# Earlier token sums for the second group and a rebuilt lead-in in a fused attention and two-MoE kernel

## The chip, the cores and the metric

One core of a Trainium2 chip. The metric is the device time of one execution in microseconds (us); lower is better. TensorE is PE in the profile (PEld is its weight load), VectorE is DVE, ScalarE is ACT, GpSimd is POOL, and SP is the engine that here only issues DMAs.

## What is computed

Attention over 2 batches and 8 heads (576 positions, 64 values per head), mixed with the answer of a compressive memory, then two feed-forward layers. All of it is fp32.

```python
# q, k, v: 2 x 8 x 576 x 64, causal
local = softmax(q @ k.T / 8, causal) @ v
mem = (phi(q) @ M_prev) / (phi(q) @ z_prev + 1e-6)     # phi(x) = elu(x) + 1
x = g * mem + (1 - g) * local                          # g = sigmoid(beta), per head
x = x.reshape(1152, 512)                               # tokens x model
x = elu(x @ w_in) @ w_out                              # 512 -> 2048 -> 512
p = probs / (probs.sum(-1) + 1e-9)                     # 1152 x 4
out = sum(p[:, e] * (relu(x @ w1[e]) @ w2[e]) for e in range(4))   # 512 -> 1024 -> 512
```

## The kernel before

**Numbers.** Every fp32 factor of a product is held as a high and a low part (fp32r), and a product is three matmuls, high times high, low times high and high times low (`mm3`, L273 to L276). Making the parts is work for the other engines: ACT copies the high part and POOL (for weights and many activations) or DVE subtracts it from the value.

**Two groups of tokens.** Group 0 has 384 tokens (the first 192 positions of both batches), group 1 has 768. The attention of group 0 is four units F0 to F3, one for each pair of heads; that of group 1 is eight units R00 to R31, one for each pair of heads and batch. Group 0 goes through both feed-forward layers with plain products: `Moe1` (tiles `ua`, `ha`, `da`) and `Moe2` (`ub`, `hb`, `db`). Group 1 goes through them as `Wide1` and `Wide2`, which save products in the first halves by working with sums of token quarters and of weight quarters. The token sums T1 to T4 of the first layer come from class `Halves`: eight DVE subtractions (L713), eight high parts on ACT (L697) and eight low parts on POOL (L700). Products with them go to PSUM banks named `pa10A`, `pa10S` and so on.

**Order in time.** The lead-in holds F0 to F3. Then group 0's `Moe1` runs on PE, with the R units interleaved, then group 0's `Moe2` and the remaining R units, then group 1.

**Weights.** Group 0's `Moe1` takes blocks 0 to 15 from a 64-bit format that is converted on the chip (`plan_weights`, L188). Each block has two halves of 512 columns. SP loads a half into a raw buffer (tags `w64_0` and `w64_1`, two buffers each), ACT works on it (`upper`, L221) and writes a PSUM bank `cv`, DVE shifts there (`shift`, L227) and combines the raw half with the bank into the fp32 tile `wr` (`lower`, L231). ACT then makes `wh` (L241), POOL makes `wl` (L245), and SP stores `wr` in DRAM for later (`keep`, L237). Block 0 (`W_EARLY = 1`) uses a bank of pool `m` and may start at once; later ones use the score banks `s0` and `s1` and wait until the last scores of F3 are issued (`GATE`).

**What sets the order.** Class `Plan` (L1033) takes every step with an engine, an estimated cost, a rank, the steps it follows and the buffers it takes and gives; `order()` sorts each engine's instructions by that. `STARTS2` sets the ranks of the R units. Where the plan expects PE to wait, `keep_busy` (L307) puts matmuls with zeros in front of a step (L300), which write a bank that the step overwrites; `FEWEST` sets a least number for the F units.

**Buffers.** Pool `ap` holds the attention's SBUF tiles, `hp0` the `h`, `ev` and `acc` tiles of group 0, `hp1` those of group 1 and the T sums with their parts. `hp1` is opened after the block that holds all of group 0, in the memory of the pools closed there.

**Small things.** `gates` (DVE, after a DMA and ACT's `gate_e`) makes g; `probs` (DVE, L137 to L140) makes p. In a unit, the local sums' quotient (L1210, L1424, L1216), the addition `both` (L1402), the transposes `turn` (L1408) and the split of the result into `xh` (L1418) and `xl` (L1416) follow one another; with F3's, the first `ua` product can start.

## Time and profile before

| what | us |
|---|---|
| median of 3 runs (734.55 to 735.07) | 734.72 |
| the profiled execution | 736.48 |
| its span in the trace | 734.70 |
| outside the span | 1.78 |
| PE busy in the span | 722.6 (98%) |
| PE idle in the span | 12.1 |

The mean granted clock of PE is 0.991 of full speed. The profiled execution was 1.76 us above the median. A stage can be read by a window: busy time of each engine in it, the granted clock and the share of time that the DMA engines worked. The stages here are the lead-in (0 to 43.6), group 0's `Moe1` (43.6 to 143.4), the rest of group 0 (to 352.15) and group 1 (to the end).

### The profile page before, as it was taken

What the parts mean: (1) busy time and instruction counts of PE and PEld (TensorE: products, weight loads), DVE (VectorE), ACT (ScalarE), POOL (GpSimd) and SP (SyncE); (2) the same over time, 40 slices, a digit from 0 to 9 for tenths busy, and PEclk for the clock granted to TensorE, in tenths of its full rate; (3) what the DMA queues carried; (4) which work ended last, traced back from release to release, by engine and by line L of the source; (5) the groups of instructions that cost most, each with busy time, mean ns of one, the idle gap of its engine ahead of it and who ended that gap; (6) DMA issues with size and microseconds to landing.
All of it is one profiled execution on the core that took longest, in us unless ns stands there. A gap on an engine that the chain in (4) does not pass through costs nothing.

```text
span 734.7 us, 11055 instructions
## 1 busy us (share of the span) xinstructions
PE 722.6 (98%) x4263; PEld 647.8 (88%) x4263; DVE 391.9 (53%) x845; ACT 352.9 (48%) x609; POOL 425.8 (58%) x256
## 2 busy tenths in 40 slices
PE   9998999999999999999899999999999999999997
PEld 5788988989788788898799999998989989899896
DVE  4675976443542443532755584864636446364562
ACT  7667877553443542443577473753424324242230
POOL 5457668756446452356998665397666456664210
PEclk9899999999999999999899999999999999999999
DMA  8378897433141230322233121212312213021002
GB/s 259 109 245 320 307 323 248 156 114 126 40 162 63 75 124 17 112 87 70 93 115 107 54 95 49 67 30 87 115 29 87 78 37 115 28 89 57 1 1 86
DMA packets 23540, 80.36 MB, mean 109 GB/s; under 512 B 2880, under 2 KB 2880, under 8 KB 23488
## 3 DMA queue, kind: packets, MB, share of 16 engines
q1 hardware_dynamic: 23488, 79.66, 32.6%
q8 instruction: 33, 0.54, 0.3%
q14 instruction: 19, 0.16, 0.1%
HBM read 68.90 MB, written 10.75 MB: 108 GB/s over the span
## 4 chain that ended last, share of the span: by engine, by line
PE 88%; DMA 4%; ACT 3%; DVE 2%; POOL 1%; issue 1%; SPq 0%; DVEq 0%; ACTq 0%
PE db L274 9%; PE db L276 9%; PE db L275 9%; PE sums L1361 5%; PE da L274 4%; PE da L276 4%; PE da L275 4%; PE ub L274 4%; DMA w<-in_w 3%; PE ub L276 3%; PE ub L275 3%; PE sR L1283 2%; PE tR L1345 2%; PE sums L1370 2%; PE sums L1231 1%; DMA wmem<-in_beta 1%
## 5 line engine op out<-in xcount | busy, mean ns | idle before, releaser
L245 POOL TENSOR_TENSOR wl<-wr,wh 128x1024 fp32r<-128x1024 f32 x72 | 171.8, 2391 | 171.5 <-ACT wh L241 124.2
L241 ACT ACTIVATE wh<-wr 128x1024 fp32r<-128x1024 f32 x72 | 75.7, 1055 | 94.2 <-PE db L275 60.8
L274 PE MATMUL db<-wh,hb 128*128 128x512 f32 x288 | 115.0, 399 | 0.0
L276 PE MATMUL db<-wl,hb 128*128 128x512 f32 x288 | 112.8, 392 | 0.0
L275 PE MATMUL db<-wh,hb 128*128 128x512 f32 x288 | 112.6, 391 | 0.0
L990 DVE SCALAR_TENSOR_TENSOR acc<-db,pr,acc 128x512 f32<-128x512 f32 x42 | 31.5, 751 | 70.0 <-PE db L276 69.2
L274 PE MATMUL da<-ha,wh 128*128 128x384 f32 x192 | 65.7, 342 | 0.0
L276 PE MATMUL da<-ha,wh 128*128 128x384 f32 x192 | 64.6, 336 | 0.8 <-POOL ha L405 0.8
L276 PEld LDWEIGHTS db<-wl,hb 128*128 128x128 f32 x288 | 54.1, 188 | 11.7
L275 PE MATMUL da<-ha,wl 128*128 128x384 f32 x192 | 64.4, 335 | 0.0
L274 PEld LDWEIGHTS db<-wh,hb 128*128 128x128 f32 x288 | 54.2, 188 | 11.0 <-issue 0.3
L275 PEld LDWEIGHTS db<-wh,hb 128*128 128x128 f32 x288 | 54.2, 188 | 10.3
L274 PE MATMUL ub<-yh,wh 128*128 128x384 f32 x128 | 45.9, 358 | 0.0
L276 PE MATMUL ub<-yl,wh 128*128 128x384 f32 x128 | 43.0, 336 | 0.0
L275 PE MATMUL ub<-yh,wl 128*128 128x384 f32 x128 | 43.0, 336 | 0.0
L1352 ACT ACTIVATE pfR<-tR 128x512 f32<-128x512 f32 x24 | 14.3, 594 | 49.3 <-PE tR L1345 49.3
L1361 PE MATMUL sums<-rvR,pfR 128*128 128x65 f32 x288 | 37.5, 271 | 0.0
L533 DVE SCALAR_TENSOR_TENSOR acc<-db,pr,acc 128x512 f32<-128x512 f32 x21 | 15.8, 751 | 40.4 <-PE db L276 40.1
L276 PEld LDWEIGHTS da<-ha,wh 128*128 128x128 f32 x192 | 36.0, 188 | 1.5 <-POOL ha L405 1.4
L502 ACT ACTIVATE hb<-ub 128x384 fp32r<-128x384 f32 x32 | 15.7, 491 | 43.7 <-PE ub L276 43.7
L274 PEld LDWEIGHTS da<-ha,wh 128*128 128x128 f32 x192 | 36.1, 188 | 0.6 <-issue 0.2
L1361 PEld LDWEIGHTS sums<-rvR,pfR 128*128 128x128 f32 x288 | 35.3, 191 | 1.2 <-DVE tmR L1216 0.2
(881 smaller groups left out, 1880.0 us busy)
## 6 DMA issues: line engine op xcount, KB each, us to landing
wr<-in_w SPq DMA_DIRECT2D x64, 512.0 KB, 3.5
w<-in_w SPq DMA_DIRECT2D x32, 512.0 KB, 5.8
wscr<-wr SPq DMA_DIRECT2D x16, 512.0 KB, 7.0
wr<-wscr SPq DMA_DIRECT2D x16, 512.0 KB, 3.4
qkR<-in_qk_r SPq DMA_DIRECT2D x8, 480.0 KB, 5.2
rvR<-in_vm_r SPq DMA_DIRECT2D x8, 390.0 KB, 3.1
out<-acc SPq DMA_DIRECT2D x8, 256.0 KB, 2.0
qkF<-in_qk_f SPq DMA_DIRECT2D x4, 416.0 KB, 3.6
```

The lines of the kernel that those rows point to most:

```text
L241: nc.scalar.activation(out=t["wh"], in_=t["wr"], func=AF.Copy)
L245: nc.gpsimd.tensor_tensor(out=wl, in0=t["wr"], in1=f32(t["wh"]), op=ALU.subtract)
L274: nc.tensor.matmul(out, ah, bh, start=first, stop=False)
L275: nc.tensor.matmul(out, al, bh, start=False, stop=False)
L276: nc.tensor.matmul(out, ah, bl, start=False, stop=last)
L502: nc.scalar.activation(out=t["h"][:, 0], in_=t["ps"], func=AF.Relu)
L533: nc.vector.scalar_tensor_tensor(out=acc, in0=t["ps"], scalar=p, in1=acc, op0=ALU.mult, op1=ALU.add)
L990: nc.vector.scalar_tensor_tensor(out=acc, in0=t["ps"], scalar=p, in1=acc, op0=ALU.mult, op1=ALU.add)
L1283: nc.tensor.matmul(unit["s", odd, t, n][:, :w], unit[x][rows, q], unit[y][rows, ks[odd]], start=m == 0 and r0 == 0, stop=m == 2 and final,)
L1345: nc.tensor.transpose(pst[:, P * n:P * n + P], src, ident)
L1361: nc.tensor.matmul(unit["ov"][:, odd, t], pf[:, col:col + P], unit["rv"][:, at_], start=j == 0, stop=False)
L1370: nc.tensor.matmul(unit["ov"][r0:r0 + r, o, t], pf[rows, col + r0:col + r0 + r], unit["rv"][rows, at_], start=nb == 0, stop=True,)
```

## The change

**Second group's sums.** `attention_pools` puts pool `ap` on a stack of its own. When the first T sum is emitted, `second_pools` closes `ap` and opens `hp1` in its memory. The T steps are in the first plan now: they need only the R units' results (`join_l`) and have a rank shortly behind the last R unit's start. `hp0` stays open to the end under the name `low`; tiles `m1`, `u2`, `u3` and `u4` of the Wide layers use four of its `h` buffers.

**Lead-in.** `W_EARLY` is 3: blocks 0 to 2 do not wait for F3's scores, and their conversion takes place in the `wr` tile itself (SBUF) and takes no bank. There are three raw buffers for each half. R units have earlier ranks. `gates` comes behind F0's memory and score steps, and `probs` behind the first output tile of `Moe1`'s last part. F0's split of q and k is in two pieces. The memory product of an F unit comes behind the sums of the unit ahead. A least number of dummy matmuls stands ahead of every score block but t = 1, where it was only ahead of the first.

```diff
-        plan.add(("gate_e",), "act", 0.4, later, gate_e, [("load_gate",)])
-        plan.add(("gates",), "dve", 0.3, later, gates, [("gate_e",)])
+        plan.add(("gate_e",), "act", 0.4, later, gate_e, [("load_gate",), ("F0", "phi_p")])
+        plan.add(("gates",), "dve", 0.3, later, gates, [("gate_e",), ("F0", "lowest101")])
-        plan.add(("probs",), "dve", 1.0, 30.0, setup_probs, [("load_probs",)])
+        plan.add(("probs",), "dve", 1.0, 30.0, setup_probs, [("load_probs",), ("a0", "d", 2, 0, 0)])
-    W_EARLY = 1
+    W_EARLY = 3
-        "wr": 3, "w64_0": 2, "w64_1": 2, "w": NW, "h": 5, "ev": 3,
+        "wr": 3, "w64_0": 3, "w64_1": 3, "w": NW, "h": 5, "ev": 3,
-    STARTS2 = [12, 45, 75, 95, 110, 125, 140, 155]
+    STARTS2 = [0, 35, 70, 95, 110, 125, 140, 155]
-            t["cv", half] = abank("m" if i < W_EARLY else f"s{half}", f"cv{i}_{half}")
+            if i < W_EARLY:
+                t["cv", half] = t["wr"][:, 512 * half:512 * half + 512]
+            else:
+                t["cv", half] = abank(f"s{half}", f"cv{i}_{half}")
...
-                            self.acc = hp[0].tile([P, 4, NTOK[self.g]], F32, tag="acc", name=f"xr{self.g}", bufs=1)
+                            self.acc = low.tile([P, 4, NTOK[self.g]], F32, tag="acc", name=f"xr{self.g}", bufs=1)
...
         def total(self, name, kk, fn):
+            second_pools()
...
-                kept[what, f] = hp[0].tile([P, 384], F32, tag=what, name=f"{what}{self.name}{part}{f}", bufs=SLOTS[what])
+                kept[what, f] = keep[what].bitcast(F32)[:, f if SLOTS[what] == 2 else 0]
...
+        pieces = [("0", slice(0, nq)), ("", slice(nq, nq + nk))] if uid == "F0" else [("", slice(0, nq + nk))]
...
-        add("mem", "pe", mem_cost, mem, ["phi", "load_v"], ["om"], ["pp"])
+        before = [(f"F{c - 1}", "sum_f")] if kind == "F" and c else []
+        add("mem", "pe", mem_cost, mem, ["phi", "load_v", *before], ["om"], ["pp"])
-            keep_busy(unit["s", 0, t, n], FEWEST[kind] * (n == t == 0))
+            keep_busy(unit["s", 0, t, n], FEWEST[kind] * (t != 1))
...
+    hp[0] = low = ctx.enter_context(tc.tile_pool(name="hp0", bufs=SLOTS["h"], reuse_waits="tile"))
+    attention = ExitStack()
+    def second_pools():
+        if hp[0] is low:
+            attention.close()
+            hp[0] = ctx.enter_context(tc.tile_pool(name="hp1", bufs=4, reuse_waits="tile"))
+            for name in ("T1", "T3", "T2", "T4"):
+                for part in "hl":
+                    x1.tile(name, part)
     with ExitStack() as first, tc.manual_schedule():
-        attention_pools(first)
+        attention_pools(attention, first)
-        hp[0] = first.enter_context(tc.tile_pool(name="hp0", bufs=SLOTS["h"], reuse_waits="tile"))
...
+        x1.plan(plan, START2 + STARTS2[-1] + 8.0, lambda name, kk: [(f"R{b}{c}", "join_l") for b, c in units])
         free = plan.order({"pe": 0.43 * WARM - 0.5})
...
-        for tile_ in ("T1", "T3", "T2", "T4"):
-            for part in "hl":
-                x1.tile(tile_, part)
-        x1.plan(plan, clock[0] - 40.0, lambda name, kk: [])
+        for what in ("m1", "u2", "u3", "u4"):
+            keep[what] = low.tile([P, 2, 384], F32R, tag="h", name=what)
```

The same work stands in another order on the engines, so the rows below are from the programs. A name with a number is a tile; line numbers of after are up to 14 higher (L227 is L231, L231 is L235, L713 and L697 are L718 and L702).

SP's queue in the lead-in, from the load of block 1's second half on. `w_2_0` is the first half of block 2, `rvF` the values of a unit F, `wscr<-wr` a stored block. Before:

```order
L211 DMA w_1_1_319<-in_w 128x512
L1161 DMA rvF_351<-in_vm_f 128x650
L1161 DMA rvF_447<-in_vm_f 128x650
L211 DMA w_2_0_477<-in_w 128x512
L211 DMA w_2_1_513<-in_w 128x512
L237 DMA wscr<-wr_367 128x1024
L211 DMA w_3_0_637<-in_w 128x512
L211 DMA w_3_1_654<-in_w 128x512
```

After:

```order
L211 DMA w_1_1_317<-in_w 128x512
L1168 DMA rvF_350<-in_vm_f 128x650
L211 DMA w_2_0_371<-in_w 128x512
L211 DMA w_2_1_414<-in_w 128x512
L1168 DMA rvF_444<-in_vm_f 128x650
L211 DMA w_3_0_482<-in_w 128x512
L211 DMA w_3_1_525<-in_w 128x512
L241 DMA wscr<-wr_366 128x1024
```

Both halves of blocks 2 and 3 stand ahead of the first stored block now.

DVE around F3's sums, the end of the lead-in: `nv_F` and the first `tvF` are the quotient of the local sums, the second `tvF` is `both`, whose transposes the first `ua` needs. Before:

```order
L231 SCALAR_TENSOR_TENSOR wr_569<-w_1_0_267,cv_0_570 128x512
L1416 TENSOR_TENSOR xl_101<-xF_614,xh_100 128x384
L1350 COPY pfF_642<-tF_622 128x384
L227 TENSOR_SCALAR cv_1_597<-cv_1_597 128x512
L231 SCALAR_TENSOR_TENSOR wr_569<-w_1_1_319,cv_1_597 128x512
L227 TENSOR_SCALAR cv_0_640<-cv_0_640 128x512
L1210 SCALAR_TENSOR_TENSOR nv_F_658<-sums,wloc 128x6
L1424 RECIPROCAL nv_F_658<-nv_F_658 128x6
L1216 TENSOR_TENSOR tvF_661<-sums,nv_F_658 128x2x3x64
L1402 TENSOR_TENSOR tvF_661<-tvF_661,sums 128x384
L231 SCALAR_TENSOR_TENSOR wr_639<-w_2_0_477,cv_0_640 128x512
```

After:

```order
L231 TENSOR_SCALAR wr_550<-wr_550 128x512
L1364 COPY pfF_654<-tF_644 128x384
L1430 TENSOR_TENSOR xl_101<-xF_639,xh_100 128x384
L235 SCALAR_TENSOR_TENSOR wr_550<-w_2_0_371,wr_550 128x512
L231 TENSOR_SCALAR wr_550<-wr_550 128x512
L1223 SCALAR_TENSOR_TENSOR nv_F_673<-sums,wloc 128x6
L1438 RECIPROCAL nv_F_673<-nv_F_673 128x6
L1229 TENSOR_TENSOR tvF_676<-sums,nv_F_673 128x2x3x64
L1416 TENSOR_TENSOR tvF_676<-tvF_676,sums 128x384
L235 SCALAR_TENSOR_TENSOR wr_550<-w_2_1_414,wr_550 128x512
```

Ahead of F3's sums DVE has worked on blocks 0 and 1 and most of block 2 now, in SBUF (`wr_550` is block 2's tile); before it had blocks 0 and 1 and one shift of block 2, in banks.

ACT near the end of group 0, from the last token part (`xB22h`) on; `hb` is the activation of `Moe2`'s last part, `wh48A` and `swh48S` are the Wide weights' first high parts. Before:

```order
L1418 ACTIVATE xB22h<-xR_3590 128x384
L241 ACTIVATE wh_3640<-wr_3563 128x1024
L606 ACTIVATE wh48A_3773<-wr_3762 128x1024
L502 ACTIVATE hb_3643<-ub_3644 128x384
L502 ACTIVATE hb_3659<-ub_3660 128x384
```

After:

```order
L1432 ACTIVATE xB22h<-xR_3578 128x384
L702 ACTIVATE xT1h<-xT_3609 128x384 x2
L702 ACTIVATE xT2h<-xT_3626 128x384 x2
L702 ACTIVATE xT3h<-xT_3634 128x384 x2
L702 ACTIVATE xT4h<-xT_3656 128x384 x2
L245 ACTIVATE wh_3666<-wr_3551 128x1024
L610 ACTIVATE wh48A_3790<-wr_3781 128x1024
L506 ACTIVATE hb_3669<-ub_3670 128x384
L610 ACTIVATE swh48S_3795<-s_48_0_3787 128x1024
L610 ACTIVATE wh48A_3798<-wr_3783 128x512
L506 ACTIVATE hb_3685<-ub_3686 128x384
```

The eight high parts of T1 to T4 stand ahead of `hb` and of the last plain weights. On POOL the eight low parts stand likewise ahead of the last plain `wl`, with the weight sums between them.

In counts, PE's dummy matmuls ahead of `da` go from 18 to none, ahead of F units' scores (`sF`) from 7 to 13, ahead of their transposes (`tF`) from 10 to 8, ahead of R units' scores (`sR`) from none to 4, and ahead of `ua` from 5 to 7, two of them later in the stage.

## Rows read from the trace of the kernel before

**Rows 1.** The page: engines' busy time, and TensorE's clock in 40 slices.

```profile
PE 722.6 (98%) x4263; PEld 647.8 (88%) x4263; DVE 391.9 (53%) x845; ACT 352.9 (48%) x609; POOL 425.8 (58%) x256
PEclk9899999999999999999899999999999999999999
```

**Rows 2.** Waits of PE: engine, line, what ended it, us, times, longest.

```profile
PE pa10S L276 <- POOL xT2l L700: 1.6, 2, 1.1
PE ua L274 <- ACT xr L440: 1.3, 1, 1.3
PE sR L1283 <- DVE wr L231: 1.2, 1, 1.2
...
PE sF L300 <- DVE nmF L1297: 0.8, 1, 0.8
PE da L276 <- POOL ha L405: 0.8, 2, 0.5
PE sums L300 <- DVE tvF L1216: 0.7, 1, 0.7
PE pa10S L276 <- POOL xT3l L700: 0.5, 1, 0.5
```

**Rows 3.** Windows: start:end, length, busy PE, PEld, DVE, ACT, POOL, PEclk, DMA, GB/s.

```profile
30.00:40.00 10.00, 9.34 (x71) 7.32 (x69) 6.43 (x21) 4.11 (x10) 1.37 (x2) 0.66 0.26 91
...
60.00:70.00 10.00, 8.75 (x51) 8.00 (x52) 4.10 (x9) 6.60 (x13) 8.06 (x5) 1.00 1.02 400
...
100.00:120.00 20.00, 18.84 (x134) 17.35 (x135) 13.56 (x33) 11.98 (x21) 16.38 (x10) 1.00 0.92 332
...
360.00:380.00 20.00, 19.51 (x95) 18.70 (x95) 15.30 (x30) 16.08 (x33) 19.92 (x14) 0.83 0.23 81
```

**Rows 4.** Timeline of the hand-over: start, us, engine, line, operation, [idle before].

```profile
330.45 0.56 DVE L1416 TENSOR_TENSOR xB22l<-xR,xB22h 128x384 fp32r<-128x384 f32 x1
...
337.29 2.41 POOL L245 TENSOR_TENSOR wl<-wr,wh 128x1024 fp32r<-128x1024 f32 x1 [6.45 <-ACT wh L241]
337.55 1.06 ACT L606 ACTIVATE wh48A<-wr 128x1024 fp32r<-128x1024 f32 x1 [0.34 <-PE db L275]
...
339.82 0.49 ACT L502 ACTIVATE hb<-ub 128x384 fp32r<-128x384 f32 x1 [1.21 <-PE ub L276]
...
343.61 0.34 PE L276 MATMUL ub<-yl,wh 128*128 128x384 f32 x1
...
353.02 1.03 DVE L713 TENSOR_TENSOR xT<-x 128x384 f32<-128x384 f32 x2
...
355.36 1.33 POOL L700 TENSOR_TENSOR xT1l<-xT,xT1h 128x384 fp32r<-128x384 f32 x1
355.73 1.36 DVE L713 TENSOR_TENSOR xT<-x 128x384 f32<-128x384 f32 x1
```

**Rows 5.** Dummy matmuls: duration ns min/median/max, first and last start, form.

```profile
L300 PE MATMUL da<-zeros x18: 326/326/337, 52.1 to 126.9; 128*128 128x384 bf16 x18
...
L300 PE MATMUL sF<-zeros x7: 376/379/379, 6.4 to 26.2; 128*128 128x512 bf16 x7
```

**Rows 6.** Timeline: one row of grouped dummies, with its start and length.

```profile
40.74 1.69 PE L300 MATMUL xF<-zeros 128*128 128x512 bf16 x7
```

**Rows 7.** Lines from 0 to 130: count, busy us, mean ns, idle before.

```profile
L227 DVE TENSOR_SCALAR cv<-cv 128x512 int32<-128x512 int32 x32 | 22.3, 695 | 7.8 <-ACT cv L221 7.5
L231 DVE SCALAR_TENSOR_TENSOR wr<-w,cv 128x512 int32<-128x512 int32 x32 | 21.9, 686 | 1.3
```

**Rows 8.** Timeline of the end of the lead-in, PE, DVE and ACT.

```profile
40.88 0.17 DVE L1210 SCALAR_TENSOR_TENSOR nv_F<-sums,wloc 128x6 f32<-128x6 f32 x1 [0.34 <-PE sums L1370]
...
43.63 0.47 PE L274 MATMUL ua<-xh,wh 128*128 128x384 f32 x1
```

**Rows 9.** Timeline of 14 to 17 us: DVE beside POOL.

```profile
14.23 1.96 POOL L1170 TENSOR_TENSOR qlF<-qkF,qhF 128x832 fp32r<-128x832 f32 x1
...
14.99 1.23 DVE L138 TENSOR_SCALAR prs<-prs 128x9 f32<-128x9 f32 x1
...
16.26 0.22 DVE L139 RECIPROCAL prs<-prs 128x9 f32<-128x9 f32 x1
```

**Rows 10.** Windows of PE alone: start:end, length, busy, PEclk, DMA, GB/s.

```profile
32.00:33.00 1.00, 0.58 (x4) 0.69 0.04 16
33.00:34.00 1.00, 1.00 (x12) 0.50 0.00 0
38.00:39.00 1.00, 1.00 (x7) 0.50 0.81 324
39.00:40.00 1.00, 1.00 (x9) 0.90 0.20 78
```

More of the change, by code (lines that the diff above doesn't have):

```diff
@@ L252, in plan_weights @@
                 add(f"load{half}", "sync", 1.6, lambda half=half: load64(half), [f"w64_{half}"])
-                bank = "m" if i < W_EARLY else f"s{half}"
+                bank = [] if i < W_EARLY else [f"s{half}"]
                 plan.add(
                     ("w", i, f"upper{half}"), "act", act_cost(512), rank, lambda half=half: upper(half),
-                    [last[0]] + [GATE] * (i >= W_EARLY) + [("w", i, "upper0")] * half, [bank] + ["wr"] * (half == 0),
+                    [last[0]] + [GATE] * (i >= W_EARLY) + [("w", i, "upper0")] * half, bank + ["wr"] * (half == 0),
                 )
@@ L262, in plan_weights @@
                     ends[-1], "dve", dve_cost(512), rank, lambda half=half: lower(half), [last[0]], [],
-                    [f"w64_{half}", ("m", ("w", i, f"upper{half}")) if bank == "m" else bank],
+                    [f"w64_{half}", *bank],
                 )
@@ L287, in tile_kernel, with attention_pools, pool @@
     at = {}
-    def attention_pools(stack):
-        def pool(name, **kw):
+    def attention_pools(outer, stack):
+        def pool(name, stack=stack, **kw):
             return stack.enter_context(tc.tile_pool(name=name, reuse_waits="tile", **kw))
-        at["sbuf"] = pool("ap", bufs=2)
+        at["sbuf"] = pool("ap", outer, bufs=2)
         for name in ("s", "t", "o"):
@@ L365, in products @@
                     if nb == 0 and 0 in kks:
-                        self.h[part, fc] = hp[0].tile(
+                        self.h[part, fc] = low.tile(
                             [P, 2, NTOK[self.g]], F32R, tag="h", name=f"h{self.name}{part}{fc}"
@@ L387, in exp @@
             def exp():
-                ev = hp[0].tile([P, 384], F32, tag="ev", name="ev" + "".join(map(str, key)), bufs=SLOTS["ev"])
+                ev = low.tile([P, 384], F32, tag="ev", name="ev" + "".join(map(str, key)), bufs=SLOTS["ev"])
                 t["ev"] = ev[:, :n]
@@ L518, in products @@
                     if (part, i, fcs[0]) == (0, 0, 0):
-                        self.acc = hp[0].tile([P, tiles, DM], F32, tag="acc", name=f"acc{self.g}", bufs=1)
+                        self.acc = low.tile([P, tiles, DM], F32, tag="acc", name=f"acc{self.g}", bufs=1)
                     if 0 in fcs:
@@ L722, in plan @@
                     self.plan_parts(plan, rank, name, kk, ["t32"] * kk)
+    keep = {}
     class Wide:
@@ L837, in exp @@
                 late()
-                ev = hp[0].tile([P, 384], F32, tag="ev", name="ev" + "".join(map(str, key)), bufs=SLOTS["ev"])
+                ev = low.tile([P, 384], F32, tag="ev", name="ev" + "".join(map(str, key)), bufs=SLOTS["ev"])
                 t["ev"] = ev[:, :n]
@@ L1161, in load_v, with split_h, split_l @@
             nc.sync.dma_start(out=unit["rv"], in_=vm[kind][c] if kind == "F" else vm[kind][b, c])
-        def split_h():
-            unit["h"] = atile([P, NQ + KEYS["R"]], F32R, tag="qh", name=f"qh{uid}")[:, :nq + nk]
-            nc.scalar.activation(out=unit["h"], in_=unit["k"], func=AF.Copy)
-        def split_l():
-            unit["l"] = atile([P, NQ + KEYS["R"]], F32R, tag="ql", name=f"ql{uid}")[:, :nq + nk]
+        def split_h(cs):
+            if cs.start == 0:
+                unit["h"] = atile([P, NQ + KEYS["R"]], F32R, tag="qh", name=f"qh{uid}")[:, :nq + nk]
+            nc.scalar.activation(out=unit["h"][:, cs], in_=unit["k"][:, cs], func=AF.Copy)
+        def split_l(cs):
+            if cs.start == 0:
+                unit["l"] = atile([P, NQ + KEYS["R"]], F32R, tag="ql", name=f"ql{uid}")[:, :nq + nk]
             eng = nc.vector if uid == "F0" else nc.gpsimd
-            eng.tensor_tensor(out=unit["l"], in0=unit["k"], in1=f32(unit["h"]), op=ALU.subtract)
+            eng.tensor_tensor(out=unit["l"][:, cs], in0=unit["k"][:, cs], in1=f32(unit["h"][:, cs]), op=ALU.subtract)
         def phi_r():
@@ L1191, in plan_unit @@
         add("load_v", "sync", 1.3, load_v, takes=["rv"])
-        add("split_h", "act", act_cost(nq + nk), split_h, ["load"], ["qh"])
-        eng = ("dve", dve_cost(nq + nk)) if uid == "F0" else ("pool", pool_cost(nq + nk))
-        add("split_l", *eng, split_l, ["split_h"], ["ql"])
+        pieces = [("0", slice(0, nq)), ("", slice(nq, nq + nk))] if uid == "F0" else [("", slice(0, nq + nk))]
+        for name, cs in pieces:
+            n, first = cs.stop - cs.start, cs.start == 0
+            add("split_h" + name, "act", act_cost(n), lambda cs=cs: split_h(cs), ["load"], ["qh"] * first)
+            eng = ("dve", dve_cost(n)) if uid == "F0" else ("pool", pool_cost(n))
+            add("split_l" + name, *eng, lambda cs=cs: split_l(cs), ["split_h" + name], ["ql"] * first)
         add("phi_r", "act", act_cost(nq), phi_r, ["load"], ["pp"])
```

1 line of the change is left out of this document (removed).

## The prediction

> **What bounds the kernel now.** I read the page first. PE is busy 98% of the span and no other engine passes 58%; the clock row shows one slice below the others in the lead-in and one at the middle [rows 1]. So the end moves only by what PE does beside real work: idle time, dummy matmuls, and real work at half clock. The change leaves the products as they are, so I add up these three by stage. The list of PE's waits shows where it idles and behind whom [rows 2], and the windows show where the clock is below 1.00 [rows 3]. In the windows the reader is to multiply: busy time times (1 minus clock) is what half clock cost there. The timelines then tell which instruction was late [rows 4, 8].
>
> Three places hold nearly everything. **The hand-over** to group 1: PE waits for POOL's low parts xT2l (1.6 us in two waits) and xT3l (0.5) [rows 2], and behind that the clock in 360 to 380 is 0.83 over 19.51 us of work [rows 3], 0.17 x 19.51 = 3.3 us. **Group 0's first layer**, 43.6 to 143.4: waits of 1.3, 1.2 and 0.8 us (for ACT's xr, DVE's wr, POOL's ha) [rows 2], while the DMA engines are at 1.02 and 0.92 of their time in two windows [rows 3]; and 18 dummies [rows 5]. **The lead-in**: two waits of 0.8 and 0.7 us [rows 2]; after the second the clock falls to 0.50 at 33 and is back at 39 to 40 [rows 10]; in 30 to 40 it is 0.66 over 9.34 us [rows 3], so 0.34 x 9.34 = 3.2 us.
>
> **Part 1: the T sums right after the attention.** Before, the eight DVE subtractions start at 353.02 and their low parts on POOL at about 355 [rows 4], after PE has turned to group 1; PE waits for them. The attention's last part, xB22l, ends at 330.45 + 0.56 = 331.0, and POOL stands idle 6.45 us up to 337.29 [rows 4]. Put there, the sums are ready some ten us before use. That removes the waits, 2.1 us, and with them the fall of the clock, 3.3 us: 5.4 us.
>
> What the moved step issues: 8 subtractions on DVE, 8 high parts on ACT, 8 low parts on POOL, no DMA. Who is queued behind: on ACT the activations hb of Moe2's last part stand behind the eight high parts, one plain wh and one wh48A. A subtraction takes 1.03 us for two when POOL is quiet and 1.36 us for one when a POOL split runs beside it [rows 4]. With two other DVE instructions of about 0.75 us between them (an estimate from the two sums' length), the last sum ends between 331.0 + 8 x 0.52 + 1.5 = 336.7 and 331.0 + 8 x 1.36 + 1.5 = 343.4. Then come one high part (0.49, as hb's) and two weight parts of 1.06 [rows 4]: hb starts between 339.3 and 346.0, where it was 339.82, and PE wants its first result after the last ub at about 343.9 [rows 4]. So the cost is 0 to about 3.4 + 0.5, say 0 to 4 us. I take 1.4, nearer to the lower end: the first subtractions run before POOL has a low part to make. POOL gets 8 low parts of 1.33, 10.6 us, of which 6.45 fill its gap; the other 4 delay the weight parts, whose last one is wanted by pa10S. It has 1 to 2 us to spare by my layout, so I charge nothing; without that cover the rest, up to 2 to 3 us, would show as a wait for a POOL weight part. Net 5.4 - 1.4 = **4.0 us** (1.4 to 5.4).
>
> **Part 2: group 0's first layer.** A dummy of 512 columns costs 0.22 us, (1.69 - 0.38) / 6 from the row of seven [rows 5, 6]; one of 384 columns 0.16. The 18 ahead of da go: 2.9 us. Four ahead of R units' scores and two ahead of ua come: 1.2. Net 1.7. The dummies stood where the plan expected a wait, so part of this may come back as idle.
>
> The three waits, 3.3 us, come from weight blocks that arrive late: one for ACT's xr, which is queued behind a conversion that waits for its raw load, one for wr itself. A third raw buffer lets SP issue the loads of block 2 and 3 before the first blocks are converted and ahead of the first store; by my layout the loads from block 7 on are some 8 to 10 us sooner. DMA has room in the lead-in (0.26 in 30 to 40) [rows 3], so the work goes where there is space. I take all 3.3. What the earlier R units add: R00's second score bank waits for DVE's lowest, which I put at 1.2 us (0 to 3), the one wait for DVE in this stage being 1.2 [rows 2]. SP passes R00's two loads ahead of block 4's second half; with the third buffer that block isn't due then, so nothing. Net 1.7 + 3.3 - 1.2 = **3.8 us** (-0.5, if the waits for xr and wr stay and the bank costs 3, to 5.0).
>
> **Part 3: the lead-in.** With gates behind the first memory step DVE no longer holds F0's scores, 0.8 us; memory behind the sums of the unit ahead removes the 0.7 and the half clock, 3.2. Six dummies ahead of sF come and two ahead of tF go: 4 x 0.22 = 0.9. On PE that is 0.8 + 0.7 + 3.2 - 0.9 = 3.8 us sooner at F3's sums. But from nv_F (40.88) to ua (43.63) a chain of 2.75 us runs through DVE, PE and ACT [rows 8], and it begins on DVE, where 11 conversion instructions now stand ahead of it instead of 9. Two more cost 2 x 0.69 [rows 7] = 1.4 us.
>
> The new thing is where they work. Before, the shift reads and writes a bank and the combine reads one bank and one SBUF tile; now all is in SBUF, on three blocks. No row shows these forms, so I bound them. The nearest rows are two: a DVE instruction on 9 values beside a POOL split took 1.23 us, from 14.99 to 16.22, just past the end of that split at 16.19, while its neighbour took 0.22 [rows 9]; and the subtraction took 1.36 beside POOL instead of 0.52 [rows 4]. So an SBUF conversion can be held until a POOL instruction ends, about 1.0 us each. The other end is a gain: with nothing beside it an SBUF shift may be shorter than 0.69, at most by the whole, so 2 x 0.69 = 1.4 us would be given back. POOL was busy 1.37 us of 10 in 30 to 40 [rows 3], but the sooner weight low parts, 2.41 each [rows 4], move into it. I take one meeting at half its length, 1.2 us, as the row of light POOL load is nearest. Net 3.8 - 1.4 - 1.2 = **1.2 us** (from 3.8 - 1.4 - 9.3 = -6.9, nine instructions held 1.03 each in place of the 1.2, or -10.1 if the clock falls as before too, to 3.8). probs moves to a place where DVE has idle time; the split of F0 in two pieces costs one instruction on each of two engines that wait for the load there: nothing, and at most 0.2.
>
> The Trainium skill speaks against this part. Its page "SBUF — State Buffer", section "SBUF: two separate sides", says in my words that VectorE and GpSimd share one pair of ports as an exclusive lock held for a whole instruction, against VectorE instructions with two SBUF inputs or in a two-port mode. The rows of the nine values and of the slow subtraction [rows 4, 9] agree with it. By the rule the combines are exposed whenever POOL runs; by the bank form of before, with one SBUF input, none is. The result that it gives alone is the third rival below.
>
> **Sum.** 4.0 + 3.8 + 1.2 = 9.0 us. The profiled execution took 736.48, of which 734.70 is span and 1.78 lies around it; so 727.5. It was 1.76 above the median of the runs, 734.72; the same gain from the median gives 725.7.
>
> **Rivals.**
> *Lead-in gives back.* DVE is held a little longer, PE idles ahead of F3's turn, and the clock falls once more: 3.2 of half clock and 1.4 of further waiting lost. For it: DVE, not PE, is last before ua in my layout. Against: seven dummies stand in that gap. Gain 4.4, time 730.3.
> *The hand-over is eaten.* hb comes 4 us late instead of 1.4 and the idle time brings half clock as in 360 to 380: 2.6 + 3.3 lost, gain 3.1, 731.6. For it: eight high parts ahead of hb on ACT; against: the gap on POOL.
> *Slower: the conversions in SBUF wait for POOL.* Nine of the eleven instructions ahead of F3's sums are held about 1.03 us each: 9.3, of which 1.2 is in the sum, so 8.1 more, and 3.2 of half clock at the gap: 9.0 - 11.3 = -2.3, time 737.0. It decides from 9 us lost on the path. For it: both rows of DVE beside POOL; against: POOL runs only about a seventh of 30 to 40, and DVE had idle time in most of the lead-in (6.43 of 10 busy) [rows 3].
> *The sums don't come sooner.* The new pool lies in the attention's memory and must wait for its last readers, or POOL's queue keeps the low parts back until 355. Then part 1 falls away: gain 5.0, 729.7.
> *All goes at its best.* 5.4 + 5.0 + 3.8 = 14.2, 720.5.
>
> **How the numbers follow.** Forecast (722 to 730) 0.53; all at its best 0.11; lead-in gives back 0.15; hand-over eaten 0.09; sums not sooner 0.04; slower 0.08. About 0.2% (1.5 us) is what a measurement of this kernel can tell from no change, so faster means below 733.2. All cases but the last lie below it, and of them some 0.06 slips up to no change where two losses meet: faster 0.86, same 0.06, slower 0.08. The range leaves out the slower case at the top, half of the meeting losses, and little at the bottom: 720.0 to 733.0.
>
> **What would show it.** Part 1 is right if the xT subtractions stand at 331 to 343, PE's waits for xT2l and xT3l are gone, and the clock in the window after the hand-over is 1.00; wrong if PE waits for hb instead. Part 2: da dummies gone, no wait for xr or wr above 0.5, DMA share in the lead-in up. Part 3: first ua at about 42.4 instead of 43.63, clock 1.00 in 30 to 40; DVE instructions of the conversion at 0.7, and those beside POOL longer. The prediction is wrong if the first ua is later than 43.6, or if the idle time moves to another wait of the same length.

## The result, and the profile after

The changed kernel takes 728.13 us (median of 4 runs, 727.76 to 729.03) where the kernel before took 734.63 (734.49 to 735.07): 6.5 us less, a ratio of 0.991 with a 95% interval of 0.9896 to 0.9923. In a later comparison it took 728.14 beside 735.09. The prediction said 725.7, in 720.0 to 733.0: right in direction and within the range, 2.4 us too fast, and, as the stages show, its three terms are each off by two to three microseconds.

These are the rows of the changed kernel's page that answer to [rows 1]. PE has 5.1 us less busy time and 7.5 us less span.

```profile
PE 717.5 (99%) x4255; PEld 643.9 (89%) x4255; DVE 396.7 (55%) x846; ACT 354.2 (49%) x610; POOL 425.7 (59%) x256
PEclk9999999999999999999999999999999999999999
```

PE's waits in the changed kernel (engine, line, what ended it; us, times, longest), which answer to [rows 2]:

```profile
PE sums L1375 <- DVE pfF L1364: 2.3, 1, 2.3
PE db L280 <- POOL wl L249: 2.2, 1, 2.2
...
PE sF L304 <- DVE nmF L1311: 0.2, 1, 0.2
```

Each of the waits of [rows 2] is gone or down to 0.2: xT2l, xT3l, xr, wr, ha, tvF. Two new ones stand in their place, each longer than any of [rows 2], and neither is charged in the prediction's sum.

The windows that answer to [rows 3] (start:end, length, busy time of PE, PEld, DVE, ACT and POOL, granted clock, DMA share, GB/s):

```profile
30.00:40.00 10.00, 7.68 (x83) 6.09 (x82) 8.50 (x22) 5.23 (x11) 4.36 (x3) 1.00 0.84 303
40.00:50.00 10.00, 10.00 (x58) 7.70 (x58) 8.04 (x16) 5.57 (x9) 4.27 (x2) 0.83 0.61 194
...
60.00:70.00 10.00, 10.00 (x77) 9.54 (x75) 8.47 (x15) 8.43 (x16) 6.87 (x5) 1.00 0.81 258
...
100.00:120.00 20.00, 19.97 (x121) 18.32 (x120) 15.28 (x34) 14.42 (x25) 14.38 (x9) 1.00 0.69 241
...
340.00:360.00 20.00, 17.79 (x84) 15.75 (x84) 7.39 (x14) 8.53 (x14) 17.58 (x10) 0.91 0.41 144
360.00:380.00 20.00, 20.00 (x117) 20.00 (x117) 10.22 (x21) 14.01 (x28) 15.55 (x10) 1.00 0.31 107
```

Read them as one shift of work. DMA went from 0.26 to 0.84 in 30 to 40 and from 1.02 to 0.81 in 60 to 70: the raw loads moved into the lead-in, and PE, which was busy 8.75 of 10 in 60 to 70, is now busy all of it. The half clock left 30 to 40 and 360 to 380 and came back, shorter, in 40 to 50 and 340 to 360.

**Where the time went, stage by stage.** I had the kernel before and the changed one profiled a second time, on the same chip (e5 and e8 below). The rows that list a tile's products give the first and last start of each kind. The kernel before, then the changed kernel:

```profile
L274 PE MATMUL ua<-xh,wh x64: 334/334/469, 42.4 to 122.5; 128*128 128x384 f32 x64
...
L274 PE MATMUL ub<-yh,wh x128: 334/334/448, 141.5 to 341.4; 128*128 128x384 f32 x128
...
L274 PE MATMUL pa10A<-xB11h,wh48A x4: 334/334/335, 350.3 to 352.9; 128*128 128x384 f32 x4
```

```profile
L278 PE MATMUL ua<-xh,wh x64: 334/334/477, 44.0 to 123.6; 128*128 128x384 f32 x64
...
L278 PE MATMUL ub<-yh,wh x128: 333/334/448, 138.4 to 337.2; 128*128 128x384 f32 x128
...
L278 PE MATMUL pa10A<-xB11h,wh48A x4: 333/334/346, 350.0 to 352.6; 128*128 128x384 f32 x4
```

With the spans of 732.8 and 726.5 that makes four stages (a row's gain is before less after):

| stage | before, us | after, us | gain | forecast |
|---|---|---|---|---|
| lead-in, to the first ua | 42.4 | 44.0 | -1.6 | +1.2 |
| first ua to last ub (first layer and rest of group 0) | 299.0 | 293.2 | +5.8 | +3.8 |
| last ub to first pa10A (last products of group 0) | 8.9 | 12.8 | -3.9 | -1.4 |
| group 1 | 382.5 | 376.5 | +6.0 | +5.4 |
| sum | 732.8 | 726.5 | +6.3 | +9.0 |

The first pair of profiles, of which the prediction was made from the one of before, gives -1.1, +6.5, -4.0 and +6.1. The lead-in's row depends on the pair: it also holds the zeros matmuls at the start of the program, and F0's first scores begin at 6.4 and 7.3 us in the two profiles of before, at 7.0 and 6.5 in the two of after. Counted from there the lead-in loses 0.5 in the first pair and 2.4 in the second.

**The new wait in the lead-in.** The timeline of the changed kernel around F3's sums (start, us, engine, line, operation, [idle before]):

```profile
36.41 2.36 POOL L249 TENSOR_TENSOR wl<-wr,wh 128x1024 fp32r<-128x1024 f32 x1 [2.18 <-ACT wh L245]
...
37.31 1.74 DVE L231 TENSOR_SCALAR wr<-wr 128x512 int32<-128x512 int32 x1
38.98 0.55 DVE L1364 COPY pfF<-tF 128x384 f32<-128x384 f32 x1
...
39.58 0.44 PE L1375 MATMUL sums<-rvF,pfF 128*128 128x65 f32 x2 [2.32 <-DVE pfF L1364]
...
40.51 0.42 DVE L231 TENSOR_SCALAR wr<-wr 128x512 int32<-128x512 int32 x1
...
40.76 3.08 PE L304 MATMUL xF<-zeros 128*128 128x512 bf16 x7
...
41.98 0.56 DVE L1416 TENSOR_TENSOR tvF<-tvF,sums 128x384 f32<-128x384 f32 x1
...
43.69 0.49 PE L1422 MATMUL xF<-ident,tvF 128*128 128x128 f32 x3
...
44.69 0.47 PE L278 MATMUL ua<-xh,wh 128*128 128x384 f32 x1
```

Block 2's first shift, in SBUF, takes 1.74 us: it ends at 39.05, 0.28 behind the end of POOL's low part (38.77). The same form takes 0.42 at 40.51, with POOL idle. The copy of F3's scores stands behind it on DVE, and PE stands behind the copy for 2.32 us. The half clock behind that wait falls mostly on dummies: the seven ahead of F3's transposes take 3.08 us where they took 1.69 [rows 6], and the transposes start behind them at 43.69, 1.15 after DVE has finished their input (42.54).

**The new wait ahead of group 1.** The timeline of the changed kernel there:

```profile
334.46 1.04 ACT L245 ACTIVATE wh<-wr 128x1024 fp32r<-128x1024 f32 x1
...
336.36 0.47 ACT L506 ACTIVATE hb<-ub 128x384 fp32r<-128x384 f32 x1
...
339.30 1.02 POOL L705 TENSOR_TENSOR xT4l<-xT,xT4h 128x384 fp32r<-128x384 f32 x1
340.29 2.33 POOL L249 TENSOR_TENSOR wl<-wr,wh 128x1024 fp32r<-128x1024 f32 x1
...
342.67 0.50 PE L280 MATMUL db<-wl,hb 128*128 128x512 f32 x1 [2.21 <-POOL wl L249]
```

hb, which I had priced, is in time. The late one is the last plain block's low part: its high part is ready at 335.50, but POOL takes it at 340.29, behind the T low parts and three weight sums that stood behind it before. It stood at 337.29 in [rows 4], while PE came there 5 us later.

### The profile page after: what moved, and what is told of

It is laid out like the page before. It is cut to its first block, busy times and chain, and to the rows that moved or that the text cites. A ratio compares the mean times of both kernels' runs of the same rounds, so it can differ in the third digit from the quotient of the medians.

```text
span 727.2 us, 11034 instructions
## 1 busy us (share of the span) xinstructions
PE 717.5 (99%) x4255; PEld 643.9 (89%) x4255; DVE 396.7 (55%) x846; ACT 354.2 (49%) x610; POOL 425.7 (59%) x256
## 4 chain that ended last, share of the span: by engine, by line
PE 96%; POOL 2%; DVE 1%; issue 0%; ACT 0%
PE db L278 9%; PE db L280 9%; PE db L279 9%; PE sums L1375 5%; PE da L278 5%; PE da L279 5%; PE da L280 5%; PE ub L278 3%; PE sR L1297 3%; PE ub L280 3%; PE ub L279 3%; PE tR L1359 3%; PE sums L1384 2%; PE ua L278 2%; PE ua L280 2%; PE ua L279 2%
## 5 line engine op out<-in xcount | busy, mean ns | idle before, releaser
L279 PEld LDWEIGHTS da<-ha,wl 128*128 128x128 f32 x192 | 36.1, 188 | 0.0
L1320 ACT ACTIVATE ptR<-ptR,nmR 128x576 f32<-128x576 f32 (+2 forms) x48 | 29.9, 659 | 10.2 <-DVE nmR L1311 10.2
```

The lines of the kernel that those rows point to most:

```text
L279: nc.tensor.matmul(out, al, bh, start=False, stop=False)
L1320: nc.scalar.activation(out=blk, in_=blk, func=AF.Exp, scale=-1.0, bias=unit["nm"][odd][:, k:k + 1])
```

## Experiments

**e5, the kernel before once more**, for a second profile, and **e8, the changed kernel once more**.

> The kernel before, unchanged, for a second profile. Theory: the same waits give different half clock from execution to execution; the waits of PE come out as in the rows (within 0.3 us each), but the half clock behind them doesn't cost 6.5 us in the sum again: one of its two stretches is missing or shorter, and the time is lower by that, near 733. Rival: both stretches are there at their full length whenever the waits are, and what differs between executions lies elsewhere.

Measured: 734.59 in the profiled execution, clock 0.993. The waits are the same but for sF (0.2 where it was 0.8), xr (1.0 for 1.3) and ha (0.6 for 0.8). The window rows that answer to the first and last of [rows 3], and the one ahead of the last:

```profile
30.00:40.00 10.00, 9.33 (x90) 7.38 (x88) 7.16 (x23) 4.87 (x10) 1.58 (x2) 0.83 0.29 99
...
340.00:360.00 20.00, 17.91 (x84) 14.79 (x83) 12.13 (x15) 9.59 (x17) 18.79 (x14) 0.96 0.30 100
360.00:380.00 20.00, 20.00 (x103) 19.72 (x103) 13.98 (x28) 16.84 (x34) 19.92 (x13) 0.87 0.32 102
```

The lead-in's half clock is 0.17 x 9.33 = 1.6 us behind a wait of 0.7, where the first profile had 3.2 behind the same wait. So the first half of the theory holds (another length behind the same wait), and the profile that the prediction was made from held 1.6 us more of it there than this one. At the hand-over nothing is missing: 0.04 x 17.91 and 0.13 x 20.00 are 3.3 us again. The time, expected near 733, is 1.9 below the first profile's 736.48: the first ua is 1.2 sooner, and the stage to the last ub is 0.7 shorter.

> The changed kernel, unchanged, for comparison on the same chip and for a second profile. Theory: waits of 2.3 (copy of F3) and 2.2 (last plain low part) again, half clock behind them different in length or missing, time 727 to 729. Rival: the waits themselves vary, and one of them is missing.

Measured: 728.14 (727.71 to 728.26, 4 runs), waits of 2.3 and 2.2 as before, and half clock cost 3.4 us of PE's work in both profiles. The waits repeat, as the theory says; the half clock behind them did too.

**e1, the hand-over alone.** The kernel before with `second_pools`, the T steps in the first plan and `low`:

```diff
+        x1.plan(plan, START2 + STARTS2[-1] + 8.0, lambda name, kk: [(f"R{b}{c}", "join_l") for b, c in units])
         free = plan.order({"pe": 0.43 * WARM - 0.5})
```

> The kernel before with the T sums and the second group's pool moved as in the change, and its lead-in as it was. Theory: the two halves of the change are independent, and what the trace of after shows at the hand-over is its own doing. Group 1 takes 6.1 us less from its first product to the end (382.55 to 376.42), and the last products of group 0 take 4.3 us more (8.21 to 12.51), because the last plain block's low part stands behind the T low parts on POOL: net gain 1.8, about 732.8. Rival: the low part comes late only because the new lead-in brings PE there 5 us sooner than POOL; then nothing is lost ahead of the first product of group 1, gain 6, about 728.6.

Measured: 732.1 (729.83 to 732.48), ratio 0.9958 (0.9938 to 0.9977). Group 1 takes 376.5, and PE waits 2.2 us for the low part, though its lead-in is the old one:

```profile
PE db L276 <- POOL wl L245: 2.2, 1, 2.2
```

The theory holds: the late low part is the hand-over's own doing. In this profile the clock didn't fall behind the wait, so the stage ahead of group 1 took 11.3 and not 12.8. It is the fastest of the six runs, 2.3 below their median.

**e2, the lead-in alone.** The kernel before with the rest of the diff: gates, probs, early blocks in SBUF, raw buffers, ranks, F0's pieces, the order of the memory products and the least dummies. Two of its lines:

```diff
-    W_EARLY = 1
+    W_EARLY = 3
-    STARTS2 = [12, 45, 75, 95, 110, 125, 140, 155]
+    STARTS2 = [0, 35, 70, 95, 110, 125, 140, 155]
```

> The kernel before with the new lead-in, conversions, raw buffers and ranks, and the T sums where they were. Theory: the first ua is about 1 us later (44.7), the stage to the last ub 6.7 us shorter, and the hand-over keeps its waits of 2.1 us and a clock of 0.83: gain 5.6, about 729.1. Rival: part of the shorter stage came from the place of the T sums; then the gain is 4 or less, 730.6 or more.

Measured: 731.9 (730.28 to 733.27, 9 runs), ratio 0.9957 (0.9945 to 0.997); the expectation was 2.8 too fast. The first ua is at 44.6 and the stages behind it take 294.0, 8.8 and 382.6, as expected but for 1.0 us in the first of the three. The rest of the miss is in the number that they were set against: gains read against the first profile of before, which stood 1.76 above its median, were taken off that median. By its time the run lies where the rival put it, but the rival's reason isn't borne out, since the stage to the last ub, 294.0, is within 0.8 of the full change's. The gains of e1 and e2, 2.45 and 2.65 by the medians, add up to 5.1, and the full change gives 6.5 to 7; the intervals leave room for that.

**e3, the last plain block first.**

```diff
+            weights = [("w", NW1 + NW2 - 1, part) for part in ("part_h", "part_l")] if name in ("T3", "T4") else []
-            plan.add((self.what, name + "l", kk), "pool", pool_cost(384), rank, low, [(self.what, name + "h", kk)], [], gives)
+            plan.add((self.what, name + "l", kk), "pool", pool_cost(384), rank, low, [(self.what, name + "h", kk), *weights], [], gives)
```

> The changed kernel, with the high and low parts of T3 and T4 behind the high and low part of the last plain weight block on ACT and POOL. Theory: PE's wait of 2.2 us for that low part and the half clock behind it (0.50 and 0.64 in two windows of 2 us, 1.7 us) both go, and the T parts still come in time: gain 4 over the changed kernel, about 724.2. Rival: POOL is short of time there, so the wait goes to a T part or to a weight part of group 1, and the time stays within 1.5 us of the changed kernel (726.6 to 728.1).

Measured: 728.94 (726.65 to 729.61), ratio 0.9912 (0.9887 to 0.9938): no gain. PE's first waits of that kernel:

```profile
PE pa10S L279 <- POOL swl48S L622: 2.4, 1, 2.4
PE sums L1376 <- DVE pfF L1365: 2.3, 1, 2.3
```

The rival was right, though the median lies 0.8 above its time. In the profile, the fastest of the four runs, the stage ahead of group 1 fell to 8.7, and group 1 rose to 379.1, for a weight part of its own. This order only passes the wait on, which points to POOL's load as the bound there.

**e4, block 2 held behind F3's copy.**

```diff
+                held = [("F3", "evac1")] if i == 2 else []
+                plan.add(("w", i, f"shift{half}"), "dve", dve_cost(512), rank, lambda half=half: shift(half), [last[0], *held])
```

> The changed kernel, with the two SBUF shifts of block 2 behind DVE's copy of F3's transposed scores. Theory: the wait of 2.3 us for that copy, which stood behind a shift held by POOL's low part, goes, and with it the half clock from 40 to 43.7; the first ua starts at about 42.3 where it was 44.7, and PE has no wait in the first layer: gain 2 over the changed kernel, about 726. Rival: block 2 then comes late for its products, a wait for it or dummies for that wait take it back, and the time stays at 728; or another DVE instruction stands behind a conversion held by POOL, and the first ua stays at 44.

Measured: 727.79 (726.26 to 728.62), ratio 0.9906 (0.9881 to 0.993). The timeline there:

```profile
35.68 2.36 POOL L249 TENSOR_TENSOR wl<-wr,wh 128x1024 fp32r<-128x1024 f32 x1 [2.18 <-ACT wh L245]
...
36.59 0.55 DVE L1366 COPY pfF<-tF 128x384 f32<-128x384 f32 x1
...
37.19 0.44 PE L1377 MATMUL sums<-rvF,pfF 128*128 128x65 f32 x2 [0.66 <-DVE pfF L1366]
...
37.52 0.80 DVE L231 TENSOR_SCALAR wr<-wr 128x512 int32<-128x512 int32 x1
```

The wait falls from 2.3 to 0.7 and the first ua starts at 41.7, 0.6 sooner than the theory said; in its profile the clock never falls. That confirms the cause of the wait. But the stage to the last ub is 295.1 instead of 293.2: block 2 is later, and six dummies more and a wait of 0.4 for xr came in its place. Of the 2.3 us won at the first ua the medians keep about 0.35, and the ratios to the kernel before, 0.9906 and 0.9905, nothing that these runs can tell: on the time the rival was right.

**e6, low parts of blocks 0 to 2 in quarters.**

```diff
+            for c in range(0, 1024, 256 if i < W_EARLY else 1024):
+                cs = slice(c, c + (256 if i < W_EARLY else 1024))
+                nc.gpsimd.tensor_tensor(out=wl[:, cs], in0=t["wr"][:, cs], in1=f32(t["wh"])[:, cs], op=ALU.subtract)
```

> The changed kernel, with POOL's low parts of blocks 0 to 2 in four instructions of 256 columns each, in the same place. Theory: an SBUF instruction of DVE is held until the end of the POOL instruction that runs; a quarter is about 0.6 us, so the shift that took 1.74 takes 0.4 to 1.1, the copy behind it comes some 0.6 to 1.3 sooner, and PE's wait of 2.3 falls to 1.0 to 1.7. Rival: DVE is slowed in SBUF as long as POOL works there at all, whatever the length of one instruction; then the shift keeps about 1.7 and the wait about 2.3. Time: 726.5 to 728 by the first, 728 by the second.

Measured: 727.48 (726.49 to 728.2), ratio 0.9896 (0.9879 to 0.9914). The timeline there:

```profile
36.51 2.96 POOL L251 TENSOR_TENSOR wl<-wr,wh 128x256 fp32r<-128x256 f32 x4 [2.18 <-ACT wh L245]
...
37.39 0.82 DVE L231 TENSOR_SCALAR wr<-wr 128x512 int32<-128x512 int32 x1
38.13 0.54 DVE L1366 COPY pfF<-tF 128x384 f32<-128x384 f32 x1
...
38.73 0.43 PE L1377 MATMUL sums<-rvF,pfF 128*128 128x65 f32 x2 [1.40 <-DVE pfF L1366]
```

The shift takes 0.82 where it took 1.74, although POOL works all the time around it (four instructions from 36.51 to 39.47): it ends at 38.21, about 0.2 behind the end of the second quarter. PE's wait falls to 1.4. So DVE is held to the end of the instruction that runs on POOL, not slowed while POOL is active. The rule of the Trainium skill that the prediction weighed (the page "SBUF — State Buffer", section "SBUF: two separate sides") says the same, and these two rows agree with it.

**e7, the T low parts on DVE**, with block 2 held as in e4:

```diff
+                (nc.vector if name in ("T1", "T2", "T3", "T4") else nc.gpsimd).tensor_tensor(
```

> The changed kernel with block 2's shifts held as before (the copy of F3 first), and the eight T low parts on DVE where they were on POOL. Theory: at the hand-over POOL is the bound: its 10 us of T parts are what made the last plain low part late, and when that was put first the wait went to a weight part of group 1. Without them both waits, 2.2 and 2.4, are gone, and PE has no wait between the lead-in and the end: about 724 to 724.5. Rival: DVE's subtractions with two SBUF inputs beside POOL take 1.3 each, 16 of them come late, hb's second half on DVE stands behind them, and PE waits for hb: 726 to 728.

Measured: 733.93 (732.37 to 736.98, 12 runs), ratio 0.9984 (0.9974 to 0.9993): nearly all of the gain lost. The timeline of the hand-over, DVE, POOL and PE:

```profile
338.33 2.74 POOL L249 TENSOR_TENSOR wl<-wr,wh 128x1024 fp32r<-128x1024 f32 x1 [2.00 <-ACT wh L245]
338.74 5.37 DVE L721 TENSOR_TENSOR xT<-x,xT 128x384 f32<-128x384 f32 x2
...
341.04 2.65 POOL L624 TENSOR_TENSOR wl48A<-wr,wh48A 128x1024 fp32r<-128x1024 f32 x1
...
344.03 0.55 DVE L511 SCALAR_TENSOR_TENSOR hb<-ub,hb 128x384 fp32r<-128x384 f32 x1
...
344.63 0.50 PE L280 MATMUL db<-wh,hb 128*128 128x512 f32 x1 [3.31 <-DVE hb L511]
```

The rival, and worse than its price. Two T subtractions that take 1.02 alone take 5.37: each is held to the end of a weight low part of 2.7, not of a T part of 1.3 as I had assumed. hb stands behind them, and PE behind hb for 3.3 and 1.2 us. (In this profile the clock also fell at 17 to 24 us, and its own time, 736.98, is the slowest of the twelve.)

**e9, the last plain block's low part on DVE**, one instruction, with block 2 held as in e4:

```diff
+            eng = nc.vector if i == NW1 + NW2 - 1 else nc.gpsimd
+            eng.tensor_tensor(out=wl, in0=t["wr"], in1=f32(t["wh"]), op=ALU.subtract)
```

> The changed kernel with block 2's shifts held as before (the copy of F3 first), and the low part of the last plain block on DVE where it was on POOL, behind the T sums and ahead of hb's low parts. Theory: POOL is the bound at the hand-over, and 2.3 us less on it serve both waits seen there: the last plain low part is ready by 338, and the weight parts of group 1 come 2.3 us sooner, so neither the wait of 2.2 nor that of 2.4 is left; with the lead-in of the held kernel about 724. Rival: the DVE instruction, with two SBUF inputs, is held by POOL's T parts, and PE waits 1 to 2 us for it or for hb behind it, with half clock after it: 726 to 727.5.

Measured: 724.68 (724.3 to 724.84), ratio 0.9855 (0.9838 to 0.9873) to the kernel before, 3.5 us below the changed kernel and faster than both. It holds e4's change too; beyond e4 alone the medians give 3.1. PE's two longest waits but for the start:

```profile
PE xF L1426 <- DVE tvF L1420: 0.8, 1, 0.8
PE sums L1379 <- DVE pfF L1368: 0.7, 1, 0.7
```

The moved instruction in its timeline:

```profile
334.40 1.39 DVE L250 TENSOR_TENSOR wl<-wr,wh 128x1024 fp32r<-128x1024 f32 x1 [0.88 <-ACT wh L245]
```

The theory holds. DVE makes in 1.39 what POOL makes in 2.33, at 334 instead of 340, and no wait above 0.8 is left after the start. The clock is 1.000 over the span. The stages are 41.8, 295.0, 9.5 and 376.5.

**e10, the kernel before without the dummies ahead of da.**

```diff
                             t["ps"] = ps_m.tile([P, 512], F32, tag="m", name=f"d{self.name}{part}{dc}{nb}")[:, :n]
-                            keep_busy(t["ps"])
```

> The kernel before without the 18 dummy matmuls ahead of da. Theory: they cost their own length, 18 x 0.16 = 2.9 less what turns into waiting: the stage from the first ua to the last ub gets some 1.5 to 2.9 shorter, 732 to 733. Rival: they stand where PE would wait anyway for weights; the idle time grows by their length, the stage keeps its 300 us and the time is that of before.

Measured: 734.94 (734.07 to 739.52, 10 runs), ratio 0.9996 (0.9973 to 1.0019). The stage from the first ua to the last ub takes 300.0 in its profile (299.7 and 299.0 with the dummies). Waits of 1.1 for ACT's ha, 0.4 more for POOL's ha and others stand where the dummies were. The rival was right: in its profile they cost nothing by themselves, and the interval shuts out a gain of their full 2.9 us.

**e11, two raw buffers**, and **e12, one early block**, in the changed kernel:

```diff
-        "wr": 3, "w64_0": 3, "w64_1": 3, "w": NW, "h": 5, "ev": 3,
+        "wr": 3, "w64_0": 2, "w64_1": 2, "w": NW, "h": 5, "ev": 3,
```

> The changed kernel with two raw buffers for each half (its order has 14 dummies ahead of da again, and block 2's loads stand behind rvF's). Theory: the third buffer is what brings the loads forward; without it the waits for xr and wr of the kernel before, 1 us each, are back beside the dummies' 2.2 us, and the stage from the first ua to the last ub is 3 to 5 us longer than in the changed kernel: 731 to 733. Rival: early conversion of three blocks alone is enough, the waits stay away, and only the dummies' 2.2 us come back or nothing: 728 to 730.

Measured: 730.74 (730.41 to 732.22), ratio 0.9949 (0.9929 to 0.9969). The stage to the last ub takes 296.2, 3.0 longer than with three buffers, with dummies for 2.2 of it and waits of 0.2 to 0.4. The loss lies at the lower end of the theory's size, but the waits of 1 us for xr and wr did not come back, as the rival said; the time lies between the two forecasts.

```diff
-    W_EARLY = 3
+    W_EARLY = 1
```

> The changed kernel with one early block (only block 0 is converted in SBUF; 1 and 2 go through the score banks and wait for F3's last scores), three raw buffers kept; its order has 7 dummies ahead of da and 8 ahead of R scores. Theory: no SBUF conversion stands ahead of F3's copy, so the wait of 2.3 us and the half clock behind it go and the first ua is at 42.5 or sooner; in the first layer the later blocks cost about what is won, a wait of 1 or the dummies' 1.5: 727 to 729. Rival: the early blocks are what the stage lives on; waits for weights of 2 us or more come back, and it is 730 or more.

Measured: 728.47 (727.76 to 730.47), ratio 0.9912 (0.989 to 0.9935): no difference to the changed kernel that these runs can tell. The wait of 2.3 is gone, but a wait of 1.1 for DVE's memory sums (`tmF`) stands there, with half clock from 31 to 38.7, and the first ua is at 43.8, later than the 42.5 expected; the stage to the last ub is 1.7 longer. So in that stage the two early blocks are worth 1.7 us and the third buffer 3.0, the larger part. What the early blocks are worth in the total isn't settled: the first ua is only 0.2 sooner without them, in a profile with 3.4 us of half clock in the lead-in, and the 1.7 came back in the stage ahead of group 1 (11.2 for 12.8), where the clock didn't fall this time.

## Why the prediction was right in direction and range, and off in its parts

**Direction and size.** The bound was read rightly: PE's waits, dummies and half clock, added by stage. All of the waits of [rows 2] went, and 6.5 of the 9.0 us came. The rest went to two new waits, which is the pattern of the first two rivals: the lead-in gives back, and the hand-over is eaten, each in part. Both signs came that the prediction had named for being wrong: the first ua is later than 43.6, and idle time moved to other waits of the same length. That the total still came within 2.4 us is in part luck: part 2 gave 2.0 more than forecast, while parts 1 and 3 gave 1.9 and 2.8 less.

**Part 1, 4.0 forecast, about 2.1 measured (6.0 in group 1, less 3.9 ahead of it).** The T waits went, and with them the half clock: the subtractions stood at 325.8 to 334.0, sooner than forecast, since the attention's last part ended at 325.9 where it was 331.0. The step that failed is the charge for POOL: "so I charge nothing". I had the number, 4 us more T work than the gap holds, but asked only whether the *last* weight part could bear it. In that queue the first thing behind the T parts is not a Wide weight but the last plain low part, the very row whose idle time I was filling [rows 4]. The prediction even named the size that came, "up to 2 to 3 us" as a wait for a POOL weight part, but left it out of the sum and of part 1's range. It costs 2.2 us of waiting and, in these two profiles, 1.7 of half clock. The charge that I did make, 1.4 for hb, was for an instruction that was on time; its upper end, 3.4 + 0.5, doesn't follow from the times given either, since hb's end at 346.0 + 0.5 is 2.6 behind 343.9. e3 and e9 together point to POOL's load, and not the order on it, as the bound.

The sum of part 1, 2.1 of waits and 3.3 of half clock, comes near the 6.0 of group 1, but the second term isn't shown to be a cost there. Group 1 took 382.5 us in both profiles of before, with 3.2 us of half clock in it, 382.6 in e2 with 1.7, and 382.5 in e10 with none. The last window of [rows 3] in e10:

```profile
360.00:380.00 20.00, 19.09 (x103) 17.27 (x101) 14.43 (x30) 16.74 (x33) 19.92 (x13) 1.00 0.27 84
```

There PE waited longer instead (3.0 us for the T low parts, where it was 2.1), and POOL was busy 19.92 of 20 us in both. That points to POOL's queue as what set the length of the stage, and to the 6.0 as what the late T work cost in all; that 2.1 + 3.3 comes near it is then luck. Ahead of group 1 half clock does cost: 12.7 to 12.9 us with it, 11.2 to 11.3 without, behind the same wait.

**Part 2, 3.8 forecast, 5.8 measured.** The waits for xr, wr and ha went, all of them. The charge of 1.2 for R00's score bank was for nothing: no such wait is in the trace. The prediction counted the dummies' removal as worth its length, with the note that it may come back as idle. In e10's profile it does come back, all of it, as long as the weights are late. I read dummies and waits as one loss, the late weights, which went when the loads moved into the lead-in (DMA share 0.26 to 0.84). e11 gives the third buffer 3.0 of the 5.8; e12 gives the two early blocks 1.7. These two need not add up, and no run takes apart the rest of the new lead-in (the earlier R units, gates, probs, F0's pieces, the order of the memory products, the F units' dummies).

**Part 3, +1.2 forecast, -1.6 measured.** The prediction's own test failed here: the first ua is later than 43.6 in both profiles (44.7 and 44.0). The mechanism was named, an SBUF conversion held by POOL, with rows that showed it [rows 9]; the price of one meeting at half length, 1.2, was too small and its place wrong. The meeting that counts is not ahead of F3's quotient but ahead of the copy of F3's scores, where DVE's queue puts a PE step behind it: 1.74 - 0.42 = 1.3 of holding, on top of the order that puts a conversion there at all. That PE then idles 2.3 and loses 1.7 to half clock was the first rival's loss (3.2 + 1.4), in about that size. The slower rival came true on DVE and not on PE. Five of the six SBUF shifts end 0.27 to 0.29 us behind the end of a POOL instruction, and two of the six combines 0.55 behind one; against 0.42 and 0.69 alone, seven instructions were held for 5.4 us in all (the rival had nine, for 9.3). The shifts take 1041 ns on average, where those in banks take 694. But of these meetings only the one ahead of F3's copy shows as a wait of PE; the others lie in time that DVE had to spare.

**The base.** The sum credited 6.5 us of half clock that the profiled execution held. The second profile of before, near its median, held 4.9, the 1.6 less all in the lead-in. So part of that gain was already missing in the median, and taking off the median what a slower profile shows overstates the gain, here by up to the 1.76 between the two. From the profile itself the prediction gave 727.5; the changed kernel's first profile took 729.03.

## What to carry to other kernels

When work is moved into an engine's idle gap, the price is the whole queue behind the gap and not the tightest known deadline: list each instruction behind the moved ones with the time it is wanted, and begin with the one whose arrival ended the gap. Before half clock is booked as a loss, ask who sets the pace of the stage: where PE waits for another engine anyway, it may cost nothing. Where two engines block each other in SBUF, keep the conversion off the places where a step that PE waits for stands right behind it; a single move of one instruction to the other engine (e9) can be worth more than a move of eight (e7). And count dummy matmuls as what they stand for: remove what PE would wait for, and they go with it.

## What the runs showed of the hardware

**How much half clock follows a wait isn't fixed by the wait.** The same wait of 2.2 us for the plain low part is followed by 1.6 to 1.7 us of loss to half clock in both profiles of the changed kernel and in e6, and by none in e1, e4, e11 and e12. The window 340 to 348 of e4 and of e8 (start:end, length, PE busy, clock, DMA, GB/s):

```profile
340.00:348.00 8.00, 6.50 (x29) 1.00 0.38 131
```

```profile
340.00:348.00 8.00, 6.06 (x20) 0.79 0.29 98
```

The change of e4 lies in the lead-in, not here. In one and the same kernel, that of before, the wait of 0.7 in the lead-in was followed by a loss of 3.2 in one execution and of 1.6 in another. A stretch of half clock, once it came, cost 1.6 to 1.7 us or 2.8 to 3.4; what decides between these and none stays open. It may be why times scatter, but the runs don't show it cleanly: e9, whose longest wait is 0.8, lies within 0.5 us in four runs, kernels with a wait of 2.2 to 2.4 within 0.6 (e8) to 3.0 (e2, e3).

**A shift with input and output in SBUF is faster than one in a bank, if POOL rests**: 0.42 us for 512 columns, against 0.69 in a bank [rows 7]. The prediction had a gain there as an end of its range only. It was seen once in the changed kernel, as POOL held the other five shifts. The Trainium skill's page "VectorE: DVE Perf Modes", section "Mode 2×_2P — use both read ports for one tensor", says that an instruction with one SBUF source can take two elements at a time, in fp32 too; the row, of int32, agrees. The combine, which has two sources, stays at 0.69 alone.
